# Attention and a two-layer network on one core: the product with v turned round, labels from single products, another stored order

## The chip, the cores and the metric

One core of a Trainium2 chip runs the whole kernel. The metric is the device time in microseconds (us); several runs give a median. Five engines work side by side, each through its own queue in order: TensorE (PE, with its weight loads listed as PEld), VectorE (DVE), ScalarE (ACT), GpSimd (POOL) and SyncE (SP), which here issues all the DMAs. A product on PE has a stationary operand (loaded as weights) and a moving one that is streamed past it. PE sums in PSUM banks; all else lies in SBUF.

## The reference

```python
def _attn_ref(q, k, v, centroids):            # q, k, v: 4 x 8 x 768 x 64, centroids: 8 x 16 x 64
    ...
    q_assign = np.argmax(np.einsum('bhsd,hcd->bhsc', q_n, c_n), axis=-1)
    k_assign = np.argmax(np.einsum('bhsd,hcd->bhsc', k_n, c_n), axis=-1)
    mask = q_assign[:, :, :, None] == k_assign[:, :, None, :]
    scores = scale * np.matmul(q, k.transpose(0, 1, 3, 2))
    scores = np.where(mask, scores, -1000000000.0)
    scores = scores - np.max(scores, axis=-1, keepdims=True)
    attn = np.exp(scores)
    attn = attn / (np.sum(attn, axis=-1, keepdims=True) + 1e-09)
    return np.matmul(attn, v)

def _moe_ref(x, w_in, w_out):                 # x: 3072 x 512, w_in: 512 x 2048, w_out: 2048 x 512
    h = x @ w_in
    g = np.where(h >= 1, h, np.where(h <= -1, 0.0, (h + 1) ** 2 / 4))
    return g @ w_out
```

Each query sees only the keys with the same label, that is the same nearest centroid. The heads' outputs, laid side by side, are the rows x of a network of two layers. All is float32.

## The kernel before

**Numbers.** For PE most float32 operands are split into two float16 parts, high and low, and a product is the sum of three: high with high, high with low, low with high. ACT makes the high part (`CAST`), POOL or DVE subtracts it for the low part.

**Tiling.** A batch of 768 rows is cut into 3 chunks of 256 queries; 4 batches give 12 chunks u. Within a chunk the 8 heads go in 4 pairs hp, so there are 48 pairs of heads in all. A pair has 4 score steps (two heads j, two tiles t of 128 queries). `at_scores` makes 128x768 scores on PE in tile `pair` and takes them with one DVE operation to `sS`, with the smallest per row in `sbi`. `at_soft` runs the exponential on ACT, splits it into `hl` (ACT, POOL) and sends it through a DMA transpose to `pT`, which has keys on partitions. For the first chunk of all (`whole`) it goes through PE transposes instead and stays float32. There the DMA queue is busy with loads.

**The product with v.** After the four steps `at_av` runs as one group on PE into `bank_a`: eight small products bring the reciprocal row sums `rr` (summed by the exponential, inverted by `at_sums`) to the layout of the result, with the 128x128 constant `idu` moving, and 36 products have a 128x64 part of v as weights and 256 columns of `pT` moving. The two heads of a pair take the two halves of the array. The result has features on partitions and queries along the row, which is what the network's first layer wants as its moving operand: ACT copies the row sums to `rb`, DVE multiplies, ACT and POOL split it into `X[u]`.

**Labels.** `labels` multiplies transposed q or k (weights, 128x128) by the centroids cT, 16 columns per head. cT comes in two halves a, high and low, whose products are summed in PSUM, and DVE then takes the largest.

**Network.** For each of 8 slices f of 256 hidden columns, `ffn1` runs 24 products of 256 columns (rows of the profile with `bankh`, `banki` or `bankj` from `x,w`), DVE and ACT apply the curve (`r`), ACT and POOL split it to `g`, and `ffn2` runs 12 products of 512 columns into `pair`. In the first part of the kernel w_in and w_out are also scaled and split (`w_bits`, `w_sum`, `w_split`), much of it on DVE.

**Order.** Nothing is issued as it is written. A `Recorder` takes every operation, with its dependences and a price in ns, as a node (products under one `rec.group()` are one node). `issue` runs a list scheduler forward and backward 80 times, replays each order in a small model of the machine with four phases and random delays, and keeps the best order, which is then emitted engine by engine. Therefore every row of the profile has the same line, L322 (the line that calls the recorded operation), and tiles tell them apart.

Of the kernel before, what the change touches and what calls it, by code (L numbers as in the profile page):

```python
# [10 lines left out]
F16 = mybir.dt.float16  # L11
# [24 lines left out]
PHASES = (0.0, 850.0, 1700.0, 2550.0)  # L36


LATER, LATER_DMA, SLACK = 25, 600, 20
# [5 lines left out]
ROUNDS = 80  # L45

class Recorder:
# [9 lines left out]
    def __init__(self, tc):  # L59
        self.tc, self.nc = tc, tc.nc  # L60
        self.nodes, self.seen, self.open, self.step = [], {}, None, -99
        for name in ("tensor", "scalar", "vector", "gpsimd", "sync"):
            setattr(self, name, Engine(self, name, getattr(tc.nc, name)))
# [23 lines left out]
    def price(self, eng, op, out, ins, kw):  # L87
# [11 lines left out]
        if eng == "tensor":  # L99
# [5 lines left out]
            return n / 4.8 + 3.5 if half else max(n / 2.4 + 2.5, 24)  # L105
# [25 lines left out]
    def add(self, eng, op, fn, args, kw):  # L131
# [6 lines left out]
        if node is None:  # L138
            node = Node(eng, self.step, len(self.nodes))
            self.nodes.append(node)  # L140
# [42 lines left out]
    def forward(self, prio):  # L183
# [4 lines left out]
        m = Machine(PHASES[0], slack=SLACK)  # L188
# [48 lines left out]
    def replay(self, phase):  # L237

        m = Machine(phase, Random(int(phase)))
        left = {x: len(x.preds) for x in self.nodes}  # L240
        at = dict.fromkeys(self.nodes, 0.0)
        todo = {}
        for x in reversed(self.order):
            todo.setdefault(x.eng, []).append(x)
        while todo:
            starts = []
            for e, q in todo.items():
                x = q[-1]
                if not left[x]:
                    t = max(m.clock.get(e, 0.0), at[x])  # L250
                    starts.append((max(t, m.free(x, t)), x.i))
            t, i = min(starts)
            x = self.nodes[i]
            todo[x.eng].pop()
            if not todo[x.eng]:
                del todo[x.eng]
            self.done(x, m.run(x, t), at, left, lambda y: None)
        return m.span

# [44 lines left out]

    def issue(self):
# [4 lines left out]
        best = None  # L310
        for _ in range(ROUNDS):
            self.forward(prio)
            starts = {x: x.start for x in self.nodes}
            span = sum(self.replay(p) for p in PHASES)
            if best is None or span < best[0]:
                best = span, self.order
            prio = self.backward(starts)
        span, self.order = best
# [6 lines left out]
class Machine:  # L325


    def __init__(self, phase, noise=None, slack=0):
        self.noise, self.slack = noise and noise.random, slack
# [16 lines left out]
    def run(self, x, t):  # L346

        e = x.eng
        if x.dma:
# [9 lines left out]
            if self.noise:  # L359
                end += LATER_DMA * self.noise()  # L360
            self.sent.append(end)
        else:
# [4 lines left out]
            if self.noise:  # L367
                end += LATER * self.noise()
# [19 lines left out]
class Node:  # L388
    def __init__(self, eng, step, i):
        self.eng, self.step, self.i = eng, step, i  # L390
# [5 lines left out]
class Group:  # L396
# [5 lines left out]
    def __enter__(self):  # L402
        r = self.rec
        r.open = Node("tensor", r.step, len(r.nodes))
        r.nodes.append(r.open)

    def __exit__(self, *a):
        self.rec.open = None
# [39 lines left out]
def tile_clustered_attention_moe(  # L448
# [58 lines left out]
    slots = tiles("kv", NP, 3 * 3072)  # L507
# [44 lines left out]
    idu = const.tile([P, P], F16, name="idu")  # L552
    rec.gpsimd.tensor_scalar(out=idu, in0=idf, scalar1=UNIT, scalar2=None, op0=ALU.mult)
# [64 lines left out]
    def batch_scale(b):  # L618
# [10 lines left out]
        if b == 0:  # L629
            e["sv1"] = const.tile([P, 1], F32, name="sv1")  # L630
            rec.vector.tensor_scalar(out=e["sv1"], in0=sv, scalar1=1 / UNIT, scalar2=None, op0=ALU.mult)
# [21 lines left out]
    def labels(z1, xT, n, heads):  # L653

        with rec.group():
            for i in range(n):
                for a in range(2):
                    h = heads[i]
# [645 lines left out]
```

## Time and profile before

| | |
|---|---|
| median of 3 runs | 867.04 us (865.24 to 868.2) |
| profiled execution | 869.13 us, of which the span of the profile is 867.3 |
| PE busy | 809.4 us |
| DVE, ACT, POOL busy | 650.4, 637.4, 550.1 us |
| DMA queue of SP | 80.2% of 16 engines' span, 141.30 MB |
| mean granted clock of PE | 0.984 |

The page cuts the span into 40 equal slices and gives busy tenths for each engine (9 is 90% or more). Groups are named out<-in by the program's tiles, with buffer numbers left out; behind the bar stand the busy time, the mean ns of one, and the idle time just ahead of them with what ended it. PEld rows are the weight loads. In the timeline of PE a row's length reaches into the next row, since products are pipelined; starts are exact.

### The profile page before, as it was taken

Reading aid. Unit: us, or ns where it says so; the run is one execution under the profiler, and the core shown is the slowest. Engines: PE = TensorE matmul, PEld = TensorE weight load, DVE = VectorE, ACT = ScalarE, POOL = GpSimd, SP = SyncE. Lnnn points to the kernel's source line nnn. Section 1 sums busy time; section 2 is a strip of 40 time slices with the busy share of each in tenths; the row PEclk is TensorE's granted clock in tenths of the full one; section 3 lists DMA queues with packets and bytes.
Section 4 is the critical chain, followed back from the end, with each engine's and each line's share of the span. In section 5 each row is a group of like instructions: output and inputs, shape, how many; then the busy total and the mean of one; then the engine's idle time right before and its main releaser. Section 6 shows DMA issues by size and latency. Waiting matters only on the chain.

```text
span 867.3 us, 19633 instructions
## 1 busy us (share of the span) xinstructions
PE 809.4 (93%) x7452; PEld 561.1 (65%) x7452; DVE 650.4 (75%) x1485; ACT 637.4 (73%) x1128; POOL 550.1 (63%) x527
## 2 busy tenths in 40 slices
PE   3687559999999999999999999999999999999997
PEld 3454346666767766767666766767667667676664
DVE  7999999998978868678778768678887757544322
ACT  6799888986867778678777687686776687676232
POOL 1166688876756777756766677666667577666222
PEclk9998889999999999999999999999999999999999
DMA  9985689869999979988998978998999787666100
GB/s 315 241 248 146 171 204 204 147 140 162 197 169 199 168 151 177 192 185 190 183 189 173 169 141 173 198 161 167 177 216 162 141 160 131 113 135 109 20 25 25
DMA packets 404767, 142.55 MB, mean 164 GB/s; under 512 B 372800, under 2 KB 396352, under 8 KB 404672
## 3 DMA queue, kind: packets, MB, share of 16 engines
q1 hardware_dynamic: 404672, 141.30, 80.2%
q8 instruction: 58, 0.95, 0.5%
q14 instruction: 37, 0.30, 0.1%
HBM read 40.40 MB, written 6.29 MB: 54 GB/s over the span
## 4 chain that ended last, share of the span: by engine, by line
PE 80%; DVE 12%; ACT 3%; issue 2%; DMA 2%; POOL 0%; ACTq 0%; SPq 0%; DVEq 0%; POOLq 0%
PE pair L322 40%; PE banka L322 11%; PE bankj L322 10%; PE banki L322 9%; PE bankh L322 9%; DVE sS L322 2%; DVE w L322 2%; DVE wk L322 1%; ACT w L322 1%; DMA q<-qn 1%; ACT hl L322 1%; DVE banki L322 1%; DVE qn L322 1%; ACT sS L322 1%; DVE q L322 1%
## 5 line engine op out<-in xcount | busy, mean ns | idle before, releaser
L322 POOL TENSOR_TENSOR hl<-sS,hl 128x768 f16<-128x768 f32 x176 | 299.8, 1711 | 116.0 <-ACT hl L322 83.7
L322 PE MATMUL pair<-w,g 128*128 128x512 f16 x1152 | 271.1, 379 | 0.0
L322 PEld LDWEIGHTS <-w 128*128 128x128 f16 x2304 | 223.4, 98 | 44.3 <-issue 2.6
L322 ACT ACTIVATE sS<-sS,sbi 128x768 f32<-128x768 f32 x192 | 179.3, 934 | 91.9 <-DVE sbi L322 88.6
L322 DVE CUSTOM_DVE_ANT_0 sS<-pair,zero,er 128x768 f32<-128x768 f32 x192 | 194.2, 1011 | 66.4 <-PE pair L322 41.6
L322 PEld LDWEIGHTS <-g 128*128 128x128 f16 x1152 | 110.3, 98 | 116.3 <-issue 1.6
L322 PE MATMUL pair<-kv,q 128*128 128x384 f16 x768 | 160.9, 334 | 17.6 <-DVE sbi L322 9.2
L322 ACT CAST hl<-sS 128x768 f16<-128x768 f32 x176 | 143.8, 825 | 12.9 <-DMA pT<-hl 7.9
L322 POOL TENSOR_TENSOR g<-r,g 128x512 f16<-128x512 f32 x88 | 103.7, 1179 | 63.7 <-ACT g L322 53.8
L322 PEld LDWEIGHTS <-q 128*128 128x128 f16 x1152 | 84.1, 99 | 72.8 <-issue 26.1
L322 PE MATMUL banka<-pT,kv 128*64 128x256 f16 (+1 forms) x1680 | 107.2, 282 | 0.4 <-DMA pT<-hl 0.4
L322 ACT ACTIVATE r<-r,f_ra,f_rs 128x512 f32<-128x512 f32 x88 | 71.3, 811 | 43.3 <-DVE r L322 42.5
L322 PEld LDWEIGHTS <-kv 128*64 128x64 f16 (+1 forms) x1968 | 96.9, 108 | 2.9 <-issue 1.5
L322 ACT CAST g<-r 128x512 f16<-128x512 f32 x88 | 53.8, 611 | 13.1 <-DVE r L322 10.2
L322 PE MATMUL bankh<-x,w 128*128 128x256 f16 x432 | 51.9, 273 | 0.2 <-POOL x L322 0.2
L322 POOL TENSOR_TENSOR qn<-qn,phi 128x256 f16<-128x256 f16 x48 | 34.2, 731 | 27.1 <-DVE phi L322 17.5
L322 PE MATMUL bankj<-x,w 128*128 128x256 f16 x408 | 48.3, 273 | 0.0
L322 PE MATMUL banki<-x,w 128*128 128x256 f16 x312 | 38.0, 273 | 0.0
L322 POOL TENSOR_TENSOR w<-w 128x1024 f16<-128x1024 f32 x12 | 30.2, 2513 | 10.6 <-ACT w L322 9.3
L322 PE MATMUL banki<-wk,w 128*128 128x256 f16 x312 | 36.7, 273 | 0.0
L322 ACT ACTIVATION_READ_ACCUMULATOR sS<-sS,sbi 128x1 f32 x192 | 36.0, 188 | 0.0
L322 PEld LDWEIGHTS <-ones 128*128 128x128 bf16 x256 | 18.0, 105 | 27.2 <-issue 21.6
(238 smaller groups left out, 1069.0 us busy)
## 6 DMA issues: line engine op xcount, KB each, us to landing
w<-in_moe_w_out_dram SPq DMA_DIRECT2D x14, 512.0 KB, 4.4
q<-in_q_dram SPq DMA_DIRECT2D x12, 512.0 KB, 4.9
kv<-in_k_dram SPq DMA_DIRECT2D x16, 384.0 KB, 3.8
kv<-in_v_dram SPq DMA_DIRECT2D x16, 384.0 KB, 4.4
out_dram<-o SPq DMA_DIRECT2D x11, 512.0 KB, 3.3
w<-in_moe_w_in_dram SPq DMA_DIRECT2D x10, 512.0 KB, 5.6
word<-in_moe_w_in_dram SPq DMA_DIRECT2D x6, 512.0 KB, 4.6
o<-in_v_dram SPq DMA_DIRECT2D x8, 384.0 KB, 4.5
```

The costliest lines, as they stand in the source:

```text
L322: fn(*args, **kw)
```

## The change

1. `at_av` is turned round: probabilities are stationary and v moves. v's high part gets a 65th column of ones per tile of keys, so that the row sum comes out of the product as one more column. A pair of heads runs as two groups, one for each head j, of 36 products with 128x128 weights from `pT` and 65, 64 and 65 columns. The first chunk runs in float32, 64 columns of v and apart from them one column `onef`.
2. The result now has queries on partitions. DVE adds the small constant to the row sum, inverts it and multiplies; ACT and POOL split the result to `xn`; a new DMA transpose of 128 KB per pair of heads brings it to `X[u]`. `at_sums`, `rr`, `idu`, the summing by the exponential and the copy of `rb` go.
3. `labels`, from step 22 on, multiplies both halves of cT at once (32 columns) and adds the halves with a new DVE reduction.
4. The order: replay and random delays go. 37 rounds of forward and backward are followed by a table of 137 numbers, each of which shifts the priorities of some nodes, and one last forward run. Prices of half-width products change, and a group gets 248 ns for them, though no group in the changed kernel has any.

```diff
-ROUNDS = 80
+BASE = 37
+NUDGES = (
+    1550000006, 1550000009, 1550000012, 1550000030, 1550000040, 1550000041, 1550000057, 1550000060,
...
-            return n / 4.8 + 3.5 if half else max(n / 2.4 + 2.5, 24)
+            self.tiled |= half
+            return n / 4.8 if half else max(n / 2.4 + 2.5, 25.2)
...
+        for seed in NUDGES:
+            self.nudge(seed, prio)
+        self.forward(prio)
...
-    def labels(z1, xT, n, heads):
+    def labels(xT, n, heads, tmp):
+        both = not early()
+        z1 = misc(n, 1 + both, C)
...
+                if both:
+                    rec.tensor.matmul(z1[:, i], xT[:, i], cT[:, :, h * C : (h + 1) * C], start=True, stop=True)
+                    continue
...
+        if both:
+            rec.vector.tensor_reduce(out=z, in_=zz.rearrange("p n a c -> p n c a"), op=ALU.add, axis=AX.X)
...
+        vs, e["vl"] = values(st)
+        rec.gpsimd.memset(vs[:, :, D:], 1.0)
...
         rec.scalar.activation(
-            out=sf, in_=sf, func=AF.Exp, bias=bi, scale=-1.0, accum_out=e["rs"][:, n : n + 1]
+            out=sf, in_=sf, func=AF.Exp, bias=bi, scale=-1.0
         )
...
-    def at_av(b, hp, c):
+    def at_av(b, hp, c, j):
...
+        pv = view(bank_a, [CT, 2, D + 1], F32)
         with rec.group():
             for t in range(CT):
+                if whole(b, c):
+                    runs = [
+                        [(0, D, kv["v"][:, j, kc * D : (kc + 1) * D], kc) for kc in range(T)],
+                        [(D, 1, onef, kc) for kc in range(T)],
+                    ]
+                else:
+                    runs = [[]]
+                    for kc in range(T):
+                        n = j * T + kc
+                        hi, lo = kv["vh"][:, n], kv["vl"][:, n * D : (n + 1) * D]
+                        runs[0] += [(0, D + 1, hi, kc), (0, D, lo, kc), (0, D + 1, hi, T + kc)]
+                for run in runs:
+                    for i, (x, m, w, p) in enumerate(run):
                         rec.tensor.matmul(
+                            pv[:, t, j, x : x + m], pT[:, p, t, :], w, start=(i == 0), stop=(i == len(run) - 1)
                         )
+        if j == 0:
+            return
+        rs = new("rs", [CT, 2], F32, 2)
+        rec.vector.tensor_scalar(
+            out=rs, in0=pv[:, :, :, D], scalar1=1e-9 * (UNIT if whole(b, c) else 1.0), scalar2=None, op0=ALU.add
+        )
+        rec.vector.reciprocal(rs, rs)
...
+        nat = new("xn", [2, CQ], F16)
+        rec.scalar.copy(nat[:, 0], xn)
+        rec.gpsimd.tensor_tensor(out=nat[:, 1], in0=xn, in1=nat[:, 0], op=ALU.subtract)
...
+        rec.sync.dma_start_transpose(
+            out=X[u][:, hp].rearrange("p a (t q) -> p (a t) q", q=P), in_=nat.rearrange("p a f -> p (a f)")
+        )
...
-                at(s0 + LA - 0.5, at_av, b, hp, c)
+                for j in range(2):
+                    at(s0 + LA - 2.5 + 2 * j, at_av, b, hp, c, j)
```

What stands in the queues. On PE, the first ordinary product with v of the kernel before, behind the last of the eight row-sum products (kv: v's parts as weights; 64x256 is the result's shape):

```order
L322 LDWEIGHTS rr_168
L322 MATMUL banka<-idu,rr_168 64x128
L322 LDWEIGHTS kv_61
L322 MATMUL banka<-pT_166,kv_61 64x256
L322 LDWEIGHTS kv_61
L322 MATMUL banka<-pT_164,kv_61 64x256
```

The same place now:

```order
L343 MATMUL bankh<-wk_72,ones 128x128
L343 LDWEIGHTS pT_165
L343 MATMUL banka<-kv_61,pT_165 128x65
L343 LDWEIGHTS pT_165
L343 MATMUL banka<-kv_61,pT_165 128x64
L343 LDWEIGHTS pT_165
L343 MATMUL banka<-kv_61,pT_165 128x65
```

The row-sum products are gone, and weights and moving operand have changed places.

On PE in the first chunk, before: a float32 product with v, one row for each product, the two heads' `pT` in turn, then the next pair's work.

```order
L322 LDWEIGHTS rr_167
L322 MATMUL banka<-idu,rr_167 64x128
L322 MATMUL banka<-pT_164,kv_61 64x256
L322 MATMUL banka<-pT_165,kv_61 64x256
L322 MATMUL banka<-pT_164,kv_61 64x256
```

Now, the fourth of the eight float32 groups, between the scores of two steps (`q` and `kv_63`):

```order
L343 MATMUL pair_82<-kv_63,q_68 128x384
L343 MATMUL banka<-kv_62,pT_163 128x64 x6
L343 MATMUL banka<-onef,pT_163 128x1 x6
L343 MATMUL banka<-kv_62,pT_163 128x64 x6
L343 MATMUL banka<-onef,pT_163 128x1 x6
L343 LDWEIGHTS q_68
L343 MATMUL pair_83<-kv_63,q_68 128x384
```

Each group has 24 products, 12 of them of one column, and the next scores stand behind it. The seventh and the eighth stand in the same way; the other five are followed by transposes or weight sums.

On DVE, the end of a pair of heads, before and now (ISA is the operation on the scores):

```order
L322 TENSOR_TENSOR rb_170<-banka,rb_170 128x256
L322 ISA sS_85,sbi_157<-pair_79,zero,er_148 128x768
```

```order
L343 TENSOR_SCALAR rs_167<-banka 128x4
L343 ISA sS_89,sbi_162<-pair_82,zero,er_151 128x768
L343 ISA sbi_162 128x1
L343 RECIPROCAL rs_167<-rs_167 128x4
L343 TENSOR_TENSOR rb_168<-banka,rs_167 128x256
```

The inversion now stands behind the product with v, and one scaling has come. Up to the first `r` of the network DVE has 22 score steps in its queue now and 20 before; on PE 23 steps stand ahead of the first first-layer product, against 20. On SP the 48 new transposes stand among the others:

```order
L343 DMA_TRANSPOSE pT_163<-hl_65 128x12x128
L343 DMA_TRANSPOSE x_77<-xn_169 128x4x128
L343 DMA_TRANSPOSE pT_165<-hl_67 128x12x128
```

A transpose of 4 blocks now stands between two of 12. Behind the last product with v, PE has 216 first-layer and 132 second-layer products in both orders.

More of the change, by code (lines that the diff above doesn't have):

```diff
@@ L2 @@
 from heapq import heapify, heappop, heappush
-from random import Random
 import concourse.bass as bass
@@ L235, in forward @@
         return m.span
[L237 to L258, printed above, removed]
     def backward(self, prio):
@@ L303, in backward, with nudge @@
         return start
+    def nudge(self, seed, prio):
+        a = mix(seed * 2654435761 + 1)
+        b = mix(a + 1)
+        c = mix(b + 1)
+        names = sorted({x.ev for x in self.nodes})
+        lo, every, size = b % len(names), (1, 2, 5)[(a >> 8) % 3], float(500 << ((a >> 16) % 5))
+        at = {y: i for i, y in enumerate(names)}
+        for x in self.nodes:
+            i = at[x.ev]
+            if lo <= i < lo + (1 << (a % 8)) and not (i - lo) % every:
+                r = c if c >> 8 & 1 else mix(c + i * 7919)
+                prio[x] += ((r & 0xFFFF) / 32768.0 - 1.0) * size
     def issue(self):
@@ L309, in issue @@
         prio = {x: x.step for x in self.nodes}
-        best = None
-        for _ in range(ROUNDS):
+        for _ in range(BASE):
             self.forward(prio)
[L313 to L318, printed above, removed]
+            prio = self.backward({x: x.start for x in self.nodes})
+        for seed in NUDGES:
+            self.nudge(seed, prio)
+        self.forward(prio)
         with self.tc.manual_schedule():
@@ L325, with __init__ @@
 class Machine:
-    def __init__(self, phase, noise=None, slack=0):
-        self.noise, self.slack = noise and noise.random, slack
+    def __init__(self, phase, slack):
+        self.slack = slack
         self.clock, self.bank = {}, {}
@@ L551, in tile_clustered_attention_moe @@
     idb = idf.bitcast(BF16).rearrange("p (q a) -> p q a", a=2)[:, :, 1]
-    idu = const.tile([P, P], F16, name="idu")
-    rec.gpsimd.tensor_scalar(out=idu, in0=idf, scalar1=UNIT, scalar2=None, op0=ALU.mult)
+    onef = const.tile([P, 1], F32, name="onef")
+    nc.gpsimd.memset(onef, 1.0)
     iota = const.tile([P, C], F32, name="iota")
@@ L725, in k_assign @@
         n = 2 * T
-        z1 = misc(n, C)
         kn = e["kn"]
-        mx = labels(z1, e["kT"], n, [2 * hp + i // T for i in range(n)])
+        z1, mx = labels(e["kT"], n, [2 * hp + i // T for i in range(n)], view(e["parts"][1], [n, C], F32))
         rec.vector.tensor_tensor(out=z1, in0=z1, in1=mx, op=ALU.subtract)
@@ L733, in k_assign @@
         )
-        e["k1"] = view(e["parts"][1 if b == 0 else 2], [n, P], F16)
+        e["k1"] = view(e["parts"][1], [n, P], F16)
         transpose(e["k1"], kn, pair[start()] if b == hp == 0 else None)
@@ L781, in q_assign @@
         e = Q[u]
-        z1 = misc(NQ, C)
-        mx = labels(z1, e["qT"], NQ, [i // CT for i in range(NQ)])
         zs = e["z"] = new("zs", [NQ, C], F32)
+        z1, mx = labels(e["qT"], NQ, [i // CT for i in range(NQ)], zs)
         rec.vector.tensor_tensor(out=zs, in0=z1, in1=mx, op=ALU.subtract)
```

133 lines of the change are left out of this document (54 added, 79 removed), and 17 rows, old and new, of the table NUDGES.

## The prediction

> **What bounds the kernel now.** I read the page first: busy times, slices and the chain that ended last.
>
> ```profile
> span 867.3 us, 19633 instructions
> PE 809.4 (93%) x7452; PEld 561.1 (65%) x7452; DVE 650.4 (75%) x1485; ACT 637.4 (73%) x1128; POOL 550.1 (63%) x527
> PE   3687559999999999999999999999999999999997
> DVE  7999999998978868678778768678887757544322
> PEclk9998889999999999999999999999999999999999
> PE 80%; DVE 12%; ACT 3%; issue 2%; DMA 2%; POOL 0%; ACTq 0%; SPq 0%; DVEq 0%; POOLq 0%
> ```
>
> PE is full from the ninth slice on. Before that DVE is full and PE is not, at a lowered clock, and the chain's DVE share, 12% of 867.3 or 104 us, is about as long as that head. So there are two limits, one after the other. The table by stretch says where one hands over to the other (columns: length, then busy time of PE, PEld, DVE, ACT, POOL, granted clock, DMA share, GB/s).
>
> ```profile
> 25.00:106.70 81.70, 56.99 (x509) 37.49 (x508) 77.96 (x194) 70.66 (x107) 44.26 (x36) 0.87 0.74 204
> 106.70:165.00 58.30, 47.20 (x435) 33.05 (x434) 55.90 (x113) 49.96 (x84) 49.25 (x38) 0.94 0.89 190
> 165.00:812.00 647.00, 644.64 (x6049) 448.84 (x6044) 482.68 (x1104) 484.09 (x890) 441.59 (x418) 1.00 0.87 164
> 812.00:867.30 55.30, 50.78 (x343) 33.26 (x340) 14.05 (x18) 15.31 (x22) 11.87 (x11) 0.99 0.05 20
> ```
>
> From 25 to 165 us DVE is idle 6 us in 140, and PE 36. From 165 to 812 PE is idle 2.4 us in 647. A nanosecond taken off PE there is a nanosecond off the time, as long as nothing else becomes late; work put on DVE counts only ahead of 165 us, or a little later if PE gets lighter.
>
> **The product with v.** One ordinary pair of heads on PE, in order of time (start, length, engine, what):
>
> ```profile
> 414.38 0.81 PE L322 MATMUL pair<-kv,q 128*128 128x384 f16 x4
> 415.13 0.41 PE L322 MATMUL banka<-idu,rr 128*64 128x128 f16 x8
> 415.38 2.13 PE L322 MATMUL banka<-pT,kv 128*64 128x256 f16 x36
> 417.44 0.76 PE L322 MATMUL bankj<-cT,kv 128*128 128x16 f16 x24
> 418.06 2.78 PE L322 MATMUL banki<-wk,w 128*128 128x256 f16 x24
> 420.67 0.81 PE L322 MATMUL pair<-kv,q 128*128 128x384 f16 x4
> 421.32 2.75 PE L322 MATMUL pair<-w,g 128*128 128x512 f16 x12
> ```
>
> Lengths overlap the next row, so starts are what counts. The eight row-sum products and the 36 products with v take 417.44 - 415.13 = 2.31 us. The four score products ahead of them take 0.75 us, and at 420.67 only 0.65: entering the half-width products costs 0.10. Together 2.41 us. The change puts 72 products of 65 or 64 columns there, each with 128x128 weights of its own. The trace has none of that width. From below: 24 products of 16 columns, each with its own 128x128 weights, take 0.62 us, 25.8 ns each. Along the wide ones, 24 of 256 columns take 2.61 us (108.8 ns), 4 of 384 take 0.65 (162.5): 53.7 ns for 128 columns, so 65 columns are 27.3 and a remainder of 1.4 to 2.2 ns, about 29.3. From above: if weights (25.8 less some 7 for 16 columns) and columns do not overlap, 19 + 27 = 46 ns. I take 29.3, since at 256 columns nothing of the weights shows: 72 x 29.3 = 2.11 us. Gain 0.30 us, x44 = **-13 us**; ends -24 (25.8 ns) and +40 (46 ns).
>
> A rule speaks against this. The Trainium skill, "TensorE: Matmul & The Clock Gate", section "Back-to-back issue gap", says that a stream of weight load and product pairs sustains about 81 ns per product at 128 columns. By it the 72 would take up to 5.8 us and the kernel some 150 us more, an estimate from that page. The 24 pairs in 0.62 us disagree with it.
>
> **Labels.** One product of 32 columns for two of 16. All but the first two chunks of q and the first batch of k change: 10 x 16 + 12 x 12 = 304 products saved x 25.8 ns = **-8 us**, if 32 columns cost what 16 do (from above, plus 16 x 0.42 ns each: -6).
>
> **DVE.** These rows carry what is added (columns: shapes, count | busy us, mean ns):
>
> ```profile
> L322 DVE RECIPROCAL rs<-rs 128x4 f32<-128x4 f32 x48 | 8.2, 171 | 17.8 <-ACT rs L322 17.7
> L322 DVE TENSOR_TENSOR rb<-banka,rb 128x256 f32<-128x256 f32 x44 | 18.3, 416 | 9.3 <-ACT rb L322 8.9
> L322 DVE TENSOR_REDUCE mx<-bankh 128x16 f32<-128x256 f32 x10 | 4.2, 417 | 0.8 <-PE bankh L322 0.7
> L322 DVE TENSOR_REDUCE mx<-banki 128x12 f32<-128x192 f32 x12 | 4.2, 351 | 2.0 <-PE banki L322 1.8
> ```
>
> Each pair of heads gets one small scaling (about a reciprocal, 0.17) beside the multiply and the reciprocal it had: 48 x 0.17 = 8 us, and 4 x 0.17 for the first chunk. The label sums read 512 or 384 elements: 417 and 351 ns for 256 and 192 are 1.03 ns per element, so about 0.68 and 0.55 us, 10 x 0.68 + 12 x 0.55 = 13 us. Of these 22 us, PE covers those after the handover (DVE is busy 483 of 647 us there). PE, 20 us lighter, stays ahead of DVE for longer: DVE is busy 0.75 of the full stretch, so PE falls back 0.25 us in each, and I put the handover some 65 us later, at about 230. Up to there stand some 11 pairs of heads, one chunk of q and three pairs of k: 1.9 + 0.7 + 0.7 + 1.7 = **+5 us**. Without cover all 22 would count. The order puts 23 score steps instead of 20 ahead of the first first-layer product:
>
> ```profile
> 106.73 2.78 PE L322 MATMUL bankj<-x,w 128*128 128x256 f16 x24
> ```
>
> 20 steps in 82 us from 25 to there are 4.1 us each, so I expect it 12 us later, near 119. That is work done earlier, not more; it counts nothing.
>
> **First chunk, in float32.** This is the unpriced part. Its 48 products with v in four pairs of heads become 192, with 128x128 float32 weights, half of them for one column.
>
> ```profile
> L322 PE MATMUL banka<-pT,kv 128*64 128x256 f32 x96 | 12.2, 408 | 0.0
> L322 PEld LDWEIGHTS banka<-pT,kv x96: 136/137/230, 43.8 to 101.6; 128*64 128x64 f32 x96
> 37.90 0.64 PEld L322 LDWEIGHTS pair<-idf,sS 128*128 128x128 f32 x6 [0.76 <-ACT sS L322]
> 79.26 3.94 PE L322 MATMUL banka<-pT,kv 128*64 128x256 f32 x24
> 83.79 0.42 DVE L322 TENSOR_REDUCE w_am<-bankj 128x2 f32<-128x256 f32 x1 [1.90 <-PE bankj L322]
> ```
>
> The trace shows two loads and two passes per float32 product (96 for 48). Six 128x128 float32 loads take 0.64 us, 107 ns each. At that rate a pair of heads takes 48 x 2 x 107 = 10.3 us in two blocks of 5.1; from below, 24 x 2 x 54 (half the columns) + 24 x 2 x 25.8 = 3.8 us. Before it was 12.2 / 4 = 3.1. So PE gets 4 x 0.7 to 4 x 7.2 = 3 to 29 us more; I take the upper end, as the nearest row is of the same shape. The Trainium skill, same page, section "Weight-path perf modes — Fast Weight Load (FWL) and DoubleRow", says that the fast load is not used for float32; that fits this row. PE is idle 24.7 us from 25 to 106.7, so most of it fits there, but one block of 3.94 us made DVE wait 1.90, so DVE had some 2.0 us of other work. Of the eight new blocks, the order puts five ahead of transposes or weight sums that DVE wants only later, and three (fourth, seventh and eighth) directly ahead of scores: 3 x (5.1 - 2.0) = 9, of which I take half, as scores run ahead of DVE at times: **+4 us**, ends 0 and 8 x 3.1 = 25.
>
> **Taken off ACT and POOL, added to the queue.**
>
> ```profile
> L322 ACT ACTIVATION_READ_ACCUMULATOR sS<-sS,sbi 128x1 f32 x192 | 36.0, 188 | 0.0
> L322 ACT COPY rb<-banka 128x256 f32<-128x256 f32 x48 | 17.4, 362 | 8.4 <-PE banka L322 7.5 <-POOL hl L322 0.7
> L322 ACT ACTIVATE rs<-rs 128x4 f32<-128x4 f32 x48 | 9.7, 201 | 0.2
> L322 POOL CAST rr<-rs 128x4 f16<-128x4 f32 x48 | 14.9, 311 | 10.2 <-DVE rs L322 10.0
> L322 POOL TENSOR_TENSOR rr<-rs,rr 128x4 f16<-128x4 f32 x48 | 11.9, 248 | 3.1
> q1 hardware_dynamic: 404672, 141.30, 80.2%
> L322 PE MATMUL banka<-pT,kv 128*64 128x256 f16 (+1 forms) x1680 | 107.2, 282 | 0.4 <-DMA pT<-hl 0.4
> ```
>
> ACT loses 63 us and POOL 27. Neither bounds a stage: 0, at best -3 (the chain's ACT share is 3%, 26 us, and a tenth of ACT goes). The sixteen added column-of-ones fills on POOL fall in that freed time: 0. The queue gets 48 transposes of 128 KB, 6.3 MB or 4.5% of 141.30; the share from 165 to 812 us goes from 0.87 to about 0.91. Each stands on SP behind POOL's subtraction, and the pT transposes behind it wait too. All 1680 products now wait 0.4 us for a transpose, so there is slack: 0, ends 0 and +10 (a third of a pT transpose's queue place in each of 44). The order itself I take at 0: the tail behind the last product with v holds the same 348 products before and after.
>
> **Sum.** -13 - 8 + 5 + 4 = -12 us: span 855.3, and with the 1.8 us around it 857.1 for the profiled execution, which at 869.13 was 2.1 above the median of the runs. Forecast for the median: **855 us**. What a measurement can tell from no change here is about 0.3%, 2.6 us.
>
> **Rivals.** (1) The head costs nothing: PE's 21 us all count, since DVE gets rid of its waits for ACT. For it: ACT is busy 70.66 of 81.7 us there. Against: DVE is busy 77.96. 867 - 21 - 3 = 843. (2) Slower: the float32 blocks. In half of them the clock stands at half, as it partly did at 79.26 (3.94 us against 12.2 / 4); then a pair of heads takes 15 us, PE gets 4 x 12 = 48 us more, and of this only 25 fit into its idle time. It decides from the point where PE's head is fuller than DVE's. 867 - 21 + 5 + 23 = 874. (3) The turned product saves nothing: at 33.5 ns a product, a quarter of the way from 29.3 to 46, the 72 take 2.41 us, as now, and the -13 is gone: 868. For it: no row is of that width; against: the two neighbours, 16 and 256 columns, lie on one line. (4) The queue gives back 10 us: 865. Speaking for it: share 0.87; against: 0.4 us of waits. (5) Every product waits for its whole weight load, by the row below: 72 x 98 ns = 7.1 us, 44 x 4.7 = 205 us more, 1065.
>
> ```profile
> L322 PEld LDWEIGHTS <-w 128*128 128x128 f16 x2304 | 223.4, 98 | 44.3 <-issue 2.6
> ```
>
> The 98 ns are hidden behind 109 ns products in that row, but also in the label row's 25.8, so (5) gets little. It is the strict form of what the Trainium skill's section named above says.
>
> **How the numbers follow.** Forecast (own range 849 to 861) 0.45, rival 1 0.20, rival 2 0.13, rival 3 0.12, rival 4 0.08, rival 5 0.02. Faster: 0.43 + 0.20 + a quarter of 3 and 4 = 0.68. Slower: rivals 2 and 5 and a third of 3 = 0.19. Same: 0.13. The range from 843 to 874 leaves out rival 5, the far parts of 2 and 3, and gains beyond rival 1.
>
> **What would show it.** Right: 36-product blocks of about 1.06 us start to start, label blocks of half their length, PE without idle time from some 170 us on, the first first-layer product near 119. The float32 blocks at 5 us in the head settle that term; DVE's waits for PE there are its price. Wrong if the narrow blocks last over 1.2 us, if DVE or PE shows waits for x or pT transposes in the full stretch, or if DVE is idle over 10% of the head.

## The result, and the profile after

The changed kernel takes **918.46 us** (median of four runs, 906.05 to 922.55) against 867.47 for the kernel before in the same session; the ratio is 1.0533, with a 95% interval from 1.048 to 1.0587 (the ratio leaves out one disturbed run, the median does not). The forecast was 855, with a range up to 874: the sign was wrong, and the miss is 63 us.

The page of the profile after, with the rows that answer to those of before (busy times, slices of PE, DVE and the granted clock, the chain):

```profile
span 916.0 us, 21884 instructions
PE 853.9 (93%) x8636; PEld 618.9 (68%) x8636; DVE 681.7 (74%) x1558; ACT 602.1 (66%) x840; POOL 520.6 (57%) x447
PE   3899897898999999999999899999999999999997
DVE  7866849989988886868889676878889776744322
PEclk9777757999999999999999999999999999999999
PE 68%; DVE 21%; ACT 4%; issue 3%; DMA 3%; POOL 0%; ACTq 0%; SPq 0%; DVEq 0%; POOLq 0%
```

PE has 44 us more busy time, though the change was to spare it work. In the second to the fifth slice it is now busy for 0.8 or more, where before it stood at 0.5 to 0.8 and the head belonged to DVE. The granted clock is 0.7, once 0.5, from the second to the seventh slice. The table by stretch (columns as in the prediction: length, busy time of PE, PEld, DVE, ACT, POOL, clock, DMA share, GB/s):

```profile
25.00:106.70 81.70, 77.55 (x624) 69.75 (x623) 59.70 (x157) 50.34 (x60) 22.41 (x21) 0.74 0.62 161
106.70:165.00 58.30, 45.90 (x317) 36.16 (x316) 44.03 (x84) 39.49 (x51) 32.09 (x19) 0.72 0.68 173
165.00:812.00 647.00, 621.53 (x6709) 436.74 (x6706) 520.09 (x1196) 448.77 (x639) 423.73 (x348) 0.99 0.92 172
```

Two things have changed at once. In the head PE went from 56.99 to 77.55 busy microseconds and DVE from 77.96 down to 59.70: DVE no longer sets the pace there, PE does, at a clock of 0.74 (0.87 before). Of the chain that ended last, the products with v are 44% in this stretch; before they were 9%. In the long stretch PE is idle 25.5 us where it was idle 2.4.

The head on PE, in order of time, around the first of the new float32 blocks:

```profile
33.64 1.44 PE L343 MATMUL pair<-kv,q 128*128 128x384 f16 x4
34.88 2.21 PE L343 MATMUL banka<-kv,pT 128*128 128x64 f32 x12
36.92 1.45 PE L343 MATMUL banka<-onef,pT 128*128 128x1 f32 x12
38.23 1.53 PE L343 MATMUL banka<-kv,pT 128*128 128x64 f32 x12
39.60 2.40 PE L343 MATMUL banka<-onef,pT 128*128 128x1 f32 x12
41.86 1.01 PE L343 MATMUL banki<-wk,ones 128*128 128x128 bf16 x8
```

One block of 24 products (48 instructions) takes 41.86 - 34.88 = 6.98 us, not the 5.1 of the prediction: two of the four rows of twelve stand at 1.3 us, about the 107 ns each of the nearest row, and two at 2.0 to 2.3, with a lowered clock. A product of a single column costs as much as one of 64. The fourth, the sixth and the seventh of the eight blocks (the number before the last two is the granted clock):

```profile
71.50:76.78 5.28, 5.28 (x50) 5.28 (x49) 1.36 (x3) 2.25 (x3) 2.65 (x2) 1.00 0.16 40
95.88:101.15 5.27, 5.27 (x49) 5.27 (x49) 2.52 (x4) 1.76 (x2) 3.85 (x3) 1.00 0.01 2
114.75:124.64 9.89, 9.89 (x50) 9.89 (x49) 4.85 (x12) 4.73 (x6) 5.42 (x3) 0.51 0.81 242
```

At the full clock a block takes 5.3 us, near the forecast; at half of it, 9.9. From start to start the eight take 53 us together, where eight at the full clock would take 42.

What DVE waited for in the head, from 25 to 140 us (us in total, times, longest):

```profile
DVE rs L343 <- PE banka L343: 17.2, 4, 5.2
DVE sS L343 <- PE pair L343: 9.1, 8, 6.4
```

The first row is the new scaling of the row sums. DVE takes its queue in order, and in all four pairs of heads of the first chunk this scaling stood at the front of the queue and waited for the pair's second block. In the kernel before DVE had no such wait there. The second row is the wait for scores, 6.4 us of it behind the seventh block.

The groups of the whole run (count | busy us, mean ns):

```profile
L343 PE MATMUL banka<-kv,pT 128*128 128x65 f16 x2112 | 111.9, 194 | 3.2 <-DVE rb L343 2.0 <-DMA pT<-hl 1.2
L343 PE MATMUL banka<-onef,pT 128*128 128x1 f32 x192 | 30.0, 283 | 0.0
L343 PE MATMUL banka<-kv,pT 128*128 128x64 f32 x192 | 28.3, 306 | 0.0
```

The first chunk's float32 products hold PE for 58.3 us; before, they took 12.2. An ordinary half of a pair of heads, later in the run:

```profile
403.76 1.26 PE L343 MATMUL banka<-kv,pT 128*128 128x65 f16 x36
404.87 0.81 PE L343 MATMUL pair<-kv,q 128*128 128x384 f16 x4
405.51 1.26 PE L343 MATMUL banka<-kv,pT 128*128 128x65 f16 x36
406.62 1.48 PE L343 MATMUL banki<-wk,w 128*128 128x256 f16 x12
```

Thirty-six narrow products take 1.11 us from start to start (30.7 ns each; forecast 1.06), a pair of heads 2.21 against 2.41: 0.20 us saved, 9 us of PE time in 44 pairs instead of 13.

### The profile page after: what moved, and what is told of

Its sections match the earlier page's. It is cut to its first block, busy times and chain, and to the rows that moved or that the text cites. A ratio compares the mean times of both kernels' runs of the same rounds, so it can differ in the third digit from the quotient of the medians.

```text
span 916.0 us, 21884 instructions
## 1 busy us (share of the span) xinstructions
PE 853.9 (93%) x8636; PEld 618.9 (68%) x8636; DVE 681.7 (74%) x1558; ACT 602.1 (66%) x840; POOL 520.6 (57%) x447
## 4 chain that ended last, share of the span: by engine, by line
PE 68%; DVE 21%; ACT 4%; issue 3%; DMA 3%; POOL 0%; ACTq 0%; SPq 0%; DVEq 0%; POOLq 0%
PE pair L343 32%; PE banka L343 13%; PE bankh L343 8%; PE banki L343 7%; PE bankj L343 7%; DVE sS L343 4%; DVE r L343 3%; DVE qn L343 2%; DVE banki L343 1%; DMA kv<-n 1%; DVE bankj L343 1%; DVE w L343 1%; DVE kv L343 1%; DVE mx L343 1%; DVE n L343 1%
## 5 line engine op out<-in xcount | busy, mean ns | idle before, releaser
L343 POOL TENSOR_TENSOR hl<-sS,hl 128x768 f16<-128x768 f32 x176 | 296.7, 1692 | 123.8 <-ACT hl L343 104.0
L343 PE MATMUL pair<-kv,q 128*128 128x384 f16 x768 | 165.3, 340 | 16.6 <-DVE sbi L343 13.6
L343 PE MATMUL banka<-kv,pT 128*128 128x65 f16 (+2 forms) x3360 | 140.1, 200 | 3.2 <-DVE rb L343 2.0
L343 PEld LDWEIGHTS <-q 128*128 128x128 f16 x992 | 81.7, 101 | 71.1 <-issue 28.3
L343 PEld LDWEIGHTS <-pT 128*128 128x128 f16 x3168 | 109.2, 98 | 14.7 <-issue 2.6
L343 POOL TENSOR_TENSOR xn<-rb,xn 128x256 f16<-128x256 f32 x48 | 33.2, 692 | 33.7 <-ACT xn L343 33.0
L343 POOL TENSOR_TENSOR qn<-qn,phi 128x256 f16<-128x256 f16 x48 | 31.0, 663 | 32.8 <-DVE phi L343 14.4
L343 POOL TENSOR_TENSOR w<-w 128x1024 f16<-128x1024 f32 x12 | 27.3, 2281 | 22.4 <-ACT w L343 22.3
L343 PEld LDWEIGHTS <-ones 128*128 128x128 bf16 x256 | 19.7, 112 | 22.2 <-issue 16.6
```

What stands on the lines that cost most here:

```text
L343: fn(*args, **kw)
```

## The experiments

The first theory: the float32 chunk makes PE the bound of the head. Its rivals: the stored order is a bad one, or the work that the change added makes score banks come free late. After the first four runs the question became what costs PE some 20 us in the long stretch.

**1. The float32 chunk alone taken away.** The changed kernel in its own order, where the first chunk's products read the upper 16 bits of each float32 word as bf16 (so the first chunk's values are coarser):

```diff
+ up = lambda x: x.bitcast(BF16).rearrange("p (f a) -> p f a", a=2)[:, :, 1] if whole(b, c) else x
- pv[:, t, j, x : x + m], pT[:, p, t, :], w, ...
+ pv[:, t, j, x : x + m], up(pT[:, p, t, :]), up(w), ...
```

> The changed kernel with its stored order kept instruction by instruction; only the first chunk's products with v (and the column onef) read the upper 16 bits of each float32 number, as bfloat16, so these outputs are coarser and each product is one load and one pass instead of two and two. Theory F (the float32 blocks of 5 to 9 us hold up the head, where PE was busy 77.6 of 81.7 us at a clock of 0.74): the blocks shrink to about 1 us, the first first-layer product moves from 140 us back to 110 to 118, the median falls by 25 to 35 us to 883 to 893; the idle time of PE after 165 us stays near 25 us, since the order is the same. Rival O (the stored order itself makes the head long, by putting three more score steps ahead): the first first-layer product stays at 130 or later and the median above 905.

Measured: 884.06 us, as theory F has it; the ratio to the kernel before is 1.0206, with its 95% interval in brackets here and below [1.0187, 1.0224]. By the medians the float32 form costs 34 us, by the ratios 28. The first first-layer product stands at 107.7 us (140.2 with float32, 106.7 before), and the head looks like that of before again:

```profile
25.00:106.70 81.70, 56.37 (x582) 40.61 (x580) 79.56 (x207) 68.34 (x84) 37.71 (x29) 0.82 0.85 221
```

PE 56.37, DVE 79.56. The float32 form of the first chunk is the larger half of the loss of 51 us. The idle time of PE after 165 us stayed at about 24 us.

**2. to 4. Orders made anew.** The changed kernel's operations with the scheduler of the kernel before (80 rounds) instead of the stored table; the same with the first chunk and its row sums in their old form; and the kernel before with only the new labels.

```diff
- for seed in NUDGES: self.nudge(seed, prio)
+ for _ in range(ROUNDS): ...            # 2 and 3: issue() and replay() of before
- if whole(b, c): runs = [..., [(D, 1, onef, kc) for kc in range(T)]]
+ if whole(b, c): at_av_old(b, hp, c)    # 3: rb from idu and rr, 64-row products
+ rec.vector.tensor_reduce(out=z, in_=zz..., op=ALU.add)   # 4: labels() of after
```

> The changed kernel's operations, all of them, put in order by the scheduler of before (80 rounds, each replayed with four phases and random delays, the best kept) instead of the stored table. Theory S (the stored order, tuned to one exact model, is what makes PE wait some 25 us after 165 us, in places where DVE and PE wait for each other): PE's idle time from 165 us to the last product with v falls below 6 us, the head keeps its float32 blocks, and the median is 890 to 900. Rival W (the turned product itself makes these waits, through DVE's added work or the shorter time that bank_a is free): the idle time stays at 15 us or more and the median is 910 or above.

> Turned product and single-product labels, except in the first chunk, which keeps the kernel before's form (v stationary, 256 columns of probabilities moving, row sums by the eight small products); ordered by the scheduler of before. If F and S both hold, nothing is left of the loss: the first first-layer product is at 104 to 120 us, PE is idle less than 6 us from 165 us to the last product with v, and the median is 846 to 858 (PE 9 us lighter in the product, 8 in the labels, DVE up to 5 heavier in the head). If the turned product makes the waits (W), the median is 865 to 885.

> The kernel before with only the labels changed (one product of 32 columns for two of 16 from step 22 on, and a DVE reduction that adds the halves), ordered by its own scheduler. Theory: 304 products of 25.8 ns are saved, 8 us, and DVE's 13 us of reductions lie nearly all beside a full PE: 858 to 863. Rival: the reductions stand between PE and the next step, or the order that comes out is another, and nothing is gained: 865 to 872.

Measured: 927.58 us (ratio 1.0698 [1.0617, 1.078]), 883.56 (1.0206 [1.0177, 1.0234]) and 875.21 (1.0104 [1.0086, 1.0123]). An order made anew is not better than the stored one, so the stored order is not what is wrong with the head. Between 2 and 3 the new form of the first chunk costs 44 us. PE's idle time in the long stretch stays: 27.7 us in 2, 23.6 in 3 and 8.9 in 4, against 2.4 before. So theory S fails and rival W holds in its number. The labels alone were expected to be faster and were slower: the first first-layer product came at 123.7, in a part of the run where the labels change nothing, so a new order alone moves the head by many microseconds. It also changes what is done there (24 score steps ahead of that product, 20 before), so two orders cannot be compared from a place in the middle: counted from the fourth group of 24 first-layer products on this run was 1.8 us longer than before, counted from the fifth 3.3 us shorter. That called for runs without a new order.

**5. to 8. The order held fixed.** 5 has the new labels alone, 6 the turned product alone, 7 both, 8 the float32 first chunk as well. Each operation stands where the kernel before has it, and an added one next to its neighbour. The exceptions are places where a new dependence forbids the old order: in 5 a few groups of first-layer products, in 6 some of k's steps, came to stand later.

```diff
- self.forward(prio); prio = self.backward(starts)         # scheduler
+ self.order = [self.nodes[i] for i in ORDER]              # a list written out
```

> Kernel before with the single-product labels alone, its instructions in exactly the order of the kernel before (the label sum stands directly ahead of the maximum; it is written into a part of k's tile that is free then). Theory O (the ~22 us that PE waits for are an accident of each new order): first first-layer product within 2 us of 106.7, time 859 to 863, since PE has 7 us less and nothing else moves. Theory W (the added work itself makes the score banks and transposes late): half or more of the saving is given back, 864 to 868. The run with an order of its own gave 875, 9 us of it lost ahead of the first first-layer product.

> The turned product with v alone (first chunk and labels in their old form), in exactly the order of the kernel before: the two blocks of 36 products stand where the block of rows sums and products stood, the added scaling and reciprocal directly ahead of the multiply, x's transpose directly behind POOL's subtraction. Theory O: first first-layer product within 2 us of 106.7, PE idle from 165 to 700 us under 6 us, time 856 to 862. Theory W: PE idle there 15 us or more although the order is the old one, time 868 to 880.

> Turned product with v and single-product labels, first chunk in its old form, in exactly the order of the kernel before. Theory O: 850 to 857 (both savings, 9 and 7 us, nothing given back). Theory W: 868 to 884, as the run of the same work in an order of its own gave 883.6. Between, 858 to 867, both hold in part, and the difference to 883.6 is the share of the order.

> All of the change's operations, the float32 first chunk too, in exactly the order of the kernel before. The float32 blocks cost 34 us on the stored order; if that price does not hang on the order, this is 30 to 38 us above the run of both without them. If the order that was stored eases them, it is over 40 above. Theory O for the rest: 884 to 892 in all; theory W: 900 to 920.

Measured: 886.74 (1.023 [1.019, 1.027]), 910.61 (1.0485 [1.0447, 1.0523]), 923.47 (1.0647 [1.0625, 1.0668]) and 981.74 (1.1335 [1.1274, 1.1395]). All four were slower than either theory allowed. In this order the float32 chunk costs 58 us (981.74 - 923.47). But with nearly the same sequence on PE, each product can be set against its twin of before, and the lag shows where time is lost.

In the labels' run the lag is 0.4 us at 250 us and then rises in jumps to 16. The largest, from about 0 to 5.8 us: PE of the labels' run, and PE of the kernel before at the same place (rows that say nothing here are left out).

```profile
280.59 0.56 PE L395 MATMUL bankh<-cT,q 128*128 128x32 f16 x16
282.62 2.13 PE L395 MATMUL banka<-pT,kv 128*64 128x256 f16 x36
288.46 2.72 PE L395 MATMUL bankh<-x,w 128*128 128x256 f16 x12 [3.71 <-DVE zs L395]
```

```profile
276.08 1.47 PE L322 MATMUL bankh<-x,w 128*128 128x256 f16 x12
280.64 0.95 PE L322 MATMUL bankh<-cT,q 128*128 128x16 f16 x32
283.09 2.13 PE L322 MATMUL banka<-pT,kv 128*64 128x256 f16 x36
285.15 0.82 PE L322 MATMUL pair<-kv,q 128*128 128x384 f16 x4
```

Sixteen blocks of 16 results took half of a bank of 512 numbers a row; of 32 they take all of it. Before, the first-layer half at 276.08 used the other half of bankh while the labels' block was made; now it has to stand behind that block and wait for the six steps of the labels on DVE, until 288.46. The 0.4 us saved in the label block is lost several times over. Such waits are 7.7 us in three places of the long stretch. Another 9.3 us (1.6 before) are waits for score banks, so the filled bank is not the whole price.

In the run of the turned product (6) the lag is 4.5 us at 150 us, 36.7 at 300 and 42.6 at 800. The rows at the first of its four large waits, on SP, ACT and PE:

```profile
206.03 0.38 SPq L418 DMA_DIRECT2D kv<-in_k_dram  x1
209.66 0.84 ACT L418 ACTIVATE n<-kv 128x768 f16<-128x768 f32 x1 [6.50 <-DMA kv<-in_k_dram]
210.64 0.16 PE L418 MATMUL bankh<-am,ones 128*128 128x1 bf16 x1 [4.64 <-ACT n L418]
```

In the kernel before, that load was issued at 178.48. The change exchanged the places of k's and v's raw data in the later batches (an edit that the list and the excerpt of the diff above leave out), so k of the second batch lands in the third of its buffer that the first batch's last products with v still read.

**9. to 12. The causes one by one.** 9: as 6, with the old places of k and v. 10: as 9, with x written straight, untransposed. 11: as 9, with the addition to the row sums on ACT. 12: as 9, in an order of its own.

```diff
- for a, src, n in (("k", k, 1 if b == 0 else 2), ("v", v, 2 if b == 0 else 1)):
+ for a, src, n in (("k", k, 1), ("v", v, 2)):                    # 9 to 12
- rec.sync.dma_start_transpose(out=X[u][:, hp]..., in_=nat...)    # 10
+ rec.scalar.copy(X[u][:, hp, 0], xn); rec.gpsimd.tensor_tensor(out=X[u][:, hp, 1], ...)
- rec.vector.tensor_scalar(out=rs, in0=pv[:, :, :, D], ..., op0=ALU.add)     # 11
+ rec.scalar.activation(out=rs, in_=pv[:, :, :, D], func=AF.Copy, bias=1e-9)
```

> The turned product alone in the order of the kernel before, as in the run that gave 910.6, but with k and v of the later batches in the thirds of their buffer that they had before: k's raw data does not land in the third that the last products with v of the first batch still read. In the run without this, 37 us were lost between 180 and 300 us, in four waits of 4.6 to 4.8 us for k's halves of the second batch. Theory P (the place of k's raw data makes k late): that loss goes, first-layer groups lag by under 5 us at 300 us, time 862 to 872. Theory Q (something else makes k late: the queue, or the fills on POOL): at least 20 of the 37 us stay, time 890 or more.

> As the run just described, but x's two halves are written straight into their place without the transpose by DMA, so 44 transposes of 128 KB are left out (the first layer then reads untransposed x). If the queue is what gives the products' saving back, this is 5 us or more below the run with the transposes; if x's transposes are covered, it is within 2 us of it.

> As the run with the old places of k and v, but the addition to the row sums (157 ns on DVE, 44 times, 6.9 us in all) is made by ACT, where a copy of the row sums stood before. If DVE's added work gives the saving back, 3 to 7 us below that run; if not, within 2 us, or some us above it, as ACT is busy 70% and its order is a fixed one.

> The turned product alone, k and v in their old places, in an order that the scheduler of the kernel before finds for it. Theory P: 855 to 866, as k is not late and the order is made for this work. Theory Q, or waits that any order has: 868 to 880.

Measured: 882.89 (1.0163 [1.014, 1.0186]), 865.07 (0.9971 [0.996, 0.9983]), 882.01 (1.0172 [1.0131, 1.0212]) and 880.28 (1.0139 [1.0118, 1.0159]). So in this order the places of k cost 27.7 us (910.61 - 882.89), and theory P holds for its mechanism (the lag at 300 us is 3.9); the time missed P's range, and x's transposes account for another 17.8 (882.89 - 865.07). Taking the addition off DVE gave 0.9 us, inside the intervals; in its place DVE waited 12.2 us for ACT, where it had waited 5.5 for PE, so the run says that the addition is no large cause, not that it is free. For the stretch from 165 to 812 us, 9 and then 10 (the DMA share is the number before the last):

```profile
165.00:812.00 647.00, 630.05 (x7126) 448.90 (x7125) 494.61 (x1141) 453.58 (x644) 423.53 (x345) 1.00 0.96 173
```

```profile
165.00:812.00 647.00, 641.12 (x7234) 458.50 (x7231) 497.71 (x1148) 454.89 (x647) 427.57 (x349) 1.00 0.90 165
```

Before it was 0.87. And who waits for the queue, in the same stretch of the kernel before, of 9 and of 10 (us in total, times, longest), and two of PE's waits in 9:

```profile
ACT hl L322 <- DMA pT<-hl: 7.9, 8, 1.7
```

```profile
ACT hl L418 <- DMA pT<-hl: 40.1, 40, 3.8
```

```profile
ACT hl L417 <- DMA pT<-hl: 20.2, 21, 2.7
```

```profile
PE bankh L418 <- DMA x<-xn: 3.1, 2, 2.6
PE pair L418 <- DVE sbi L418: 3.1, 5, 1.4
```

ACT may not write the next probabilities until the transposes of earlier ones have left their buffers, and PE's own waits for pT are small in all runs (0.4 us in 9). But ACT's wait is not the price by itself: in 10 it is 20.2 us, against 7.9 before, and the time is not longer. What reached PE in 9 was mostly x itself: its first layer waited 7.4 us for x's transposes (x shares its buffers with two other tiles, so this has four rows, of which one is shown), and 3.1 us for score banks, which is no more than the 4.2 of run 10.

**13. to 15. The same parts taken out of the changed kernel, in its own order.**

```diff
- rec.sync.dma_start_transpose(out=X[u]..., in_=nat...)    # 13 and 15: untransposed x
- both = not early()
+ both = False                                             # 14 and 15: old labels
+ up(pT[:, p, t, :]), up(w)                                # 15: as in 1
```

> The changed kernel in its own order, but x's halves are written straight into their place, without the 48 transposes by DMA (the first layer reads untransposed x). If x's transposes load the queue here as they did in the order of the kernel before (18 us for 44), 8 to 20 us below the changed kernel: 898 to 910. If that price belonged to a foreign order: 914 or more.

> The changed kernel in its own order, but with the labels' two products of 16 columns summed in place, and without the label sums on DVE; each block's result takes half a bank again. If the new labels save their 7 us of PE time, 920 to 926. If their sums on DVE and the whole bank give back more than they save: 905 to 916.

> The changed kernel in its own order with all three taken out: the first chunk's products with v read the upper halves of the float32 words as bf16, x is not transposed, the labels have their old form. What is left of the change is the turned product, its row sums on DVE and the places of k and v. If the three prices add up (34, 8 to 20, and the labels either way), 860 to 876. If it stays above 880, something else in the change or its order costs 15 us or more.

Measured: 913.56 (1.0486 [1.042, 1.0551]), 922.0 (1.0548 [1.0511, 1.0585]) and 888.76 (1.0234 [1.0211, 1.0258]). The first two cannot be told from the changed kernel itself (1.048 to 1.0587), and the third is not below run 1. With this order held, taking away x's transposes or the new labels gives nothing back, other than taking away the float32 form; some 20 us remain that belong to the order and the work together.

**16. The labels once more**: the old order up to about 180 us, then that of run 4.

```diff
+ P = {i: fixed[i] if fixed[i] < K else 1e5 + own[i] for i in fixed}   # rank in the old order, then in the own
```

> The kernel before with the single-product labels alone: up to the third chunk's first layer (about 180 us) in exactly the order of the kernel before, from there in the order that the run of the labels alone had, which gained 3.4 us there but lost 9 in the head. If the labels are a small gain by themselves: 861 to 866. If the gain was an accident of that order: 867 to 872.

Measured: 875.08 (1.008 [1.0063, 1.0096]). Nothing of the 3.4 us came back, which had rested on one place of comparison (above). PE waited again (636.12 us busy of the 647 from 165 to 812, against 644.64 before), and the new labels were slower in every one of the three orders they had alone.

**17. and 18. The orders crossed.** 17: the kernel before, all its own operations, in the changed kernel's order. 18: the turned product of run 10 (x untransposed, old places, old labels, old first chunk) in an order of its own.

```diff
- span, self.order = best
+ self.order = [self.nodes[i] for i in ORDER]      # 17: after's order
- rec.sync.dma_start_transpose(out=X[u]..., in_=nat...)  # 18, with 80 rounds of its own
```

> The operations of the kernel before, none changed, but in the stored order of the changed kernel (each block of row sums and products with v stands where the second block of 36 products stands there, the four small steps on the row sums shortly ahead of it). If the stored order is by itself 15 to 20 us worse in the full stretch, 880 to 895, with PE waiting for score banks as in the changed kernel. If the loss there comes from the turned product's operations alone, 867 to 874.

> The turned product without x's transposes, as in the run that gave 865.1 in the order of the kernel before, but in the order that the scheduler of the kernel before finds for it. With the transposes an order of its own gave 880.3, the old order 882.9. If the transposes are what costs there, 862 to 868. If an order made anew is worse whatever the work, 873 to 882.

Measured: 916.75 (1.0566 [1.0539, 1.0593]) and 871.14 (1.0034 [1.0017, 1.005]). Run 17 is beyond both expectations, and 18 falls between its two: unchanged operations lose 48 us in an order made for others. So a price measured in a foreign order (5 to 11, 13 to 15) is that of a stiff order, and only orders made for their own work may be compared for the net. Run 18 against 12 is such a pair: x's transposes cost 9.1 us. Here it is score banks that PE waits for; ACT's wait for the buffers is 19.7 us in 12 and 13.2 in 18. PE's waits for the score banks in the long stretch of 12, and of 18:

```profile
PE pair L336 <- DVE sbi L336: 12.2, 15, 2.1
```

```profile
PE pair L336 <- DVE sbi L336: 1.6, 3, 1.0
```

With one scheduler for all (the changed kernel's prices in all but the first), the change can be built up step by step: before 867; turned product without x's transposes 871.1; with them 880.3 (+9.1); with the new labels and the new places of k and v 883.6 (+3.3); with the float32 first chunk 927.6 (+44). The stored order then takes 9 off: 918.5. Each step is one order against one other, and how far two orders for the same work differ was not measured: the new labels alone cost 8 to 9 us in run 4, and with the places of k and v only 3.3 here. So a step of a few us is not settled; the 44 is. In the 871.1 the first first-layer product comes 9.7 us later (116.4 against 106.7), with 23 score steps ahead of it instead of 20, and the last product ends at 862.5 against 862.8: whether the 9 us that PE saves show there is not shown. No version that computes the reference beat the kernel before in these runs; 10, 13, 15 and 18 leave the transposition of x out.

## Why the prediction was wrong, point by point

- **First chunk in float32: +4 forecast, 28 to 34 us measured in the changed kernel's order, 44 between orders of their own, 58 in the order of before.** This is the step that failed. The price per product was nearly right (blocks of 5.27 and 5.28 us at the full clock, forecast 5.1), but two further steps were not. The clock: over the eight blocks it was lowered, down to 0.51 in one of 9.9 us, so PE got 58.3 - 12.2 = 46 us more instead of 29. And the cover: I let PE's idle time of 24.7 us take nearly all, and counted half of three blocks. That idle time was gaps in a chain between PE and DVE; with the blocks in it PE itself became the bound of the head (77.55 of 81.7 us busy), and DVE fell from 77.96 to 59.70. I had looked for DVE's price only where scores stand behind a block. The larger wait was elsewhere: 17.2 us at the scaling of the row sums, which needs the second block of every pair, against 9.1 for scores. Rival 2 had the clock and 48 us of added PE time, but also let 25 of it vanish into idle time.
- **The queue: 0 forecast, ends 0 and +10; 9.1 measured in orders of their own, 17.8 in the old one.** I counted bytes: 4.5% of the queue's, so a share of 0.91 in place of 0.87. In the changed kernel it is 0.92, but in run 9, with less other loss, 0.96. By the queue's share of the span (80.2% of 867.3 us before, 85.8% of 878.1 in run 9, 82.7% of 863.2 in run 10), 44 transposes took 39 to 58 us of the queue's time, where bytes gave 28. And I read slack from PE's wait for pT alone (0.4 us), not from the first layer's wait for x (7.4 us in run 9) or from the score banks (12.2 us in run 12, 1.6 in 18).
- **Labels: -8 forecast.** On PE they are there (a block of 16 products takes 0.40 us, 0.81 before). They came back as waits, in run 5 partly since a block now fills a bank; the prediction priced the sums on DVE (rightly: 0.69 us for 512 elements) and not the bank.
- **The places of k and v** had no term at all. In the old order they cost 27.7 us. What they cost in the changed kernel, whose loads of that batch's k are issued from 224.59 us on, was not measured by itself.
- **Turned product: -13 forecast, -9 measured** on PE (30.7 ns a product, not 29.3). The 0.10 us for entering half-width products did go. The ground given against rival 3, that 16 and 256 columns lie on one line, does not hold: the line of 53.7 ns for 128 columns gives 8 to 9 ns for 16, and the row has 25.8. That 65 columns came out near the line was in part luck. (Rival 5's time is, by its own terms, 1073 and not 1065.)
- **DVE: +5 forecast.** The row sums' addition cost nothing that run 11 can show. What counted was not its length but where it stands in DVE's queue (first point).
- **Order: 0 forecast.** The kernel before loses 48 us in the other order (run 17), so "the order moves nothing" was the least founded of the terms; the tail, which I had compared, says nothing of it. The stored order is 9 us better than one made anew for the same work.
- **ACT and POOL, 0:** agreed. Their busy time fell by 35 and 30 us and bought nothing; of the 63 us of ACT's rows a part had overlapped with other rows.

Of what the prediction said would prove it wrong, DVE idle over 10% of the head was there (22 of 81.7 us). The narrow blocks kept within their 1.2 us, and direct waits for transposes in the full stretch are small (PE 1.2 us for pT, none for x); yet PE is idle 25.5 us there, where the prediction had none, and the first first-layer product stands at 140.2, not 119.

What stays open: how the some 20 us that are left without the float32 form divide between transposes, labels, k's places and the order; the runs in the changed kernel's order could not tell, because the order is stiff. Why the clock falls in some blocks and not in others is open too.

## What to carry to other kernels

Before idle time of an engine is used as cover, ask whether it is slack or the gaps of a chain that runs through that engine: work put into the gaps of a chain lengthens the chain. Look in the queues of the other engines for the first operation that needs the new work, since all that stands behind it waits as well. Price a transfer by the queue time of transfers of its own kind, and look for slack at everything that waits for the queue, not only at one reader. And where an order has been fitted to its work, look in the diff for whatever changes when a buffer or a bank comes free (its size, which half, whose place): those edits look free and can cost more than the arithmetic that is saved; measure them with the old order held, and the net with an order of its own.

## What the runs showed of the hardware

- A float32 product with 128x128 stationary values takes two loads and two passes, and at the full clock a load with its pass takes about 110 ns whatever the columns moved (48 in 5.28 us; twelve in 1.31 us for one column and in 1.37 for 64). As bf16 (run 1) these products did not lengthen the head: its first first-layer product stands at 107.7 us, 106.7 in the kernel before.
- Such products came with a lower granted clock (0.74 and 0.72 in the two stretches of the head, 0.87 and 0.94 before, 0.82 and 0.90 as bf16; one slice at 0.5), but not all of them: two of the eight blocks ran at 1.00. The Trainium skill, "TensorE: Matmul & The Clock Gate", section "What's actually happening", says that the gate goes by how busy PE was of late, and that being busy releases it. Here the clock fell while PE was at its busiest (77.55 of 81.7 us), so the row does not fit that sentence as it stands; which property of these products lowers the clock was not tried.
- Narrow f16 products, each with its own 128x128 stationary values, run at 30.7 ns for 65 and 64 columns; the loads, 98 ns each in their own rows, stay hidden.
- A transpose of 128 KB by DMA takes 0.9 to 1.3 us of the queue (39 to 58 us for 44), 1.4 to 2 times its share of the bytes. The Trainium skill, "VectorE: DVE Perf Modes", section "The three transpose paths", gives such transposes some 90% of the DMA bandwidth, and 1309 ns for one 128x128 block of two bytes. A transpose here is four such blocks and took the queue no longer than the page gives for one, so that figure is not their price in a row of transfers; and measured against the queue's mean rate, not against the full bandwidth, they reached half to 70% of it. The 90% are not shown by any run here.
